# Operands split in place in a two-tile ring, and an earlier, closer-spaced preparation of the combined weights

## The chip, the cores and the metric

One NeuronCore of a Trainium2 chip runs the whole program in one launch. The metric is the device time of one execution in microseconds (us); several executions give a median. The engines are TensorE (PE, the matmuls; PEld is its weight load), VectorE (DVE), ScalarE (ACT), GpSimd (POOL) and SyncE (SP), whose queue issues nearly all DMAs.

## The reference

Three layers follow one another, all in float32: rotary attention (4 batches, 8 heads, 576 tokens, head size 64), then a layer with a maximum of three products, then one with SiLU.

```python
attn_out = _attn_ref(q, k, v)                                    # 4 x 8 x 576 x 64
x = attn_out.transpose(0, 2, 1, 3).reshape(2304, 512)
h = np.maximum(np.maximum(x @ w1, x @ w2), x @ w3)               # 512 -> 768
x = h @ w_out                                                    # 768 -> 512
h = x @ w_in                                                     # 512 -> 2048
out = (h * (1 / (1 + np.exp(-h)))) @ w_out2                      # 2048 -> 512
```

## The kernel before

A product of float32 operands is made of three float16 passes: each operand is scaled and split into a high and a low half, and the passes are high by high, high by low and low by high. ACT makes the high half, DVE the low half (`split`, L154 to L163).

**The stages.** Attention and the first layer (`moe1`) run interleaved until 610 us; then only the first layer's last batch is left, which is called the tail here: for its 576 tokens in two halves (256 and 320 columns) `up` makes 18 groups of matmuls each (3 matrices by 6 blocks of 128 hidden features), and `down` 4 groups of 18 passes each, over the 6 blocks. A group is one PSUM bank (`group`, L529). In the tail 7 banks are open to groups: 2 of `ps_m` and 5 of `ps_g`. ACT moves the first matrix's product out, DVE takes the maximum with the other two (L551, L553), ACT and DVE split the result (L559, L560), which `down` reads. `down` writes y to DRAM (`yscr`, L578).

**The second layer** (`moe2`, L827) takes tokens in 9 blocks of 256. Block 0 is computed plainly: `s1` (four units of 48 passes) makes h, `g_split` (L844) forms sums on POOL and splits, `s2` multiplies with the output weights. The other eight blocks go in four pairs J, each product of two by two sub-blocks being made from 7 products in place of 8 (`PRODUCTS`, L822). For this the operands need combined forms: sums and differences of sub-blocks. Of y they are made per J: `y7_load` (four DMAs), `y7_max` (largest magnitude, one DVE reduction), `y7_sums` (scales, and four differences on POOL, L937) and `y7_forms` (seven splits, L944, into the pool `y7_p`). `s1_pair` (8 of them, p = 0 to 7, per J) multiplies them with the combined input weights; between them stand units of `s2` (`second`).

**The combined weights** are prepared in the tail by `prep_steps` (L763), 16 items: 8 of the input weights ("wi", k = 0 to 7), 8 of the output weights ("wo", k = 8 to 15). An item loads two pieces from DRAM into a float32 tile of the ring `z7_p`, which has 3 tiles (L781); POOL makes four sums or differences in it (L785); ACT and DVE split it in two halves, forms 0 (or 1) to 3 and 4 to 7 (`high` L793, `low` L799). A "wi" item is written into a tile of the ring `w8o` (2 tiles of 8 forms) and by one DMA into DRAM (`w8scr`, L804); a "wo" item stays in SBUF as `w7`. Later `w8_load` (L1161) brings the "wi" forms back into one of four tiles, the first two of them early (L1180).

**The order.** `prep_steps` is a generator that is stepped once per group of the tail. Item k has its sums at step at0 + 3.4 k, its load 5 steps before, `high` and `low` of the first half 1 and 2 steps after, of the second 4 and 5 after; at0 is 6. Steps left at the tail's end are taken between the units of `s1` (`rest_step`). At the tail's first step block 0 of y is loaded into a tile of `z7_p` and split (L1175, L1176). A scheduler orders each engine's queue when the program is built, by this order as priority and by its own estimate of when each instruction can start; on the chip each queue runs in its order.

Of the kernel before, what the change touches and what calls it, by code (L numbers as in the profile page):

```python
# [17 lines left out]
P = 128  # L18
# [4 lines left out]
def fused_kernel(  # L23
# [502 lines left out]

    ps_g, wide_n = [], [0]

    def group(passes, n):  # L529

        wide_n[0] += 1
        ring, tag = (ps_g[0], "mg") if ps_g and wide_n[0] % 7 > 1 else (ps_m, "m")
        ps = ring.tile([P, 512], F32, tag=tag, name=tag)
        for i, (l, r) in enumerate(passes):
            nc.tensor.matmul(ps[:, 0:n], l, r, start=(i == 0), stop=(i == len(passes) - 1))  # L535
        return ps

    def moe1(b, pools):
# [33 lines left out]
        def down(half):  # L572
            o, n = PARTS[half][:2]

            def evac(m, ps):
                ysb = pools[2].tile([P, n], F32, tag="y", name="y")
                last["ma"] = nc.scalar.activation(out=ysb, in_=ps[:, 0:n], func=AF.Copy, scale=cy_t[b]).ins
                nc.sync.dma_start(out=yscr[:, m, b * S + o:b * S + o + n], in_=ysb)  # L578

            for m in range(KC):  # L580
                passes = []
                for f in range(NF1):
                    wh = WO1.h(f)[:, m * P:(m + 1) * P]
                    wl = WO1.l(f)[:, m * P:(m + 1) * P]
                    h = h1[half, f]
                    passes += [(wh, h[:, 0]), (wh, h[:, 1]), (wl, h[:, 0])]
                yield half, n * len(passes), True
                ps = group(passes, n)
                evac(m, ps)


        ahead = int(b > 0)
# [170 lines left out]
    def prep_steps(stage, out_p, w7_p, w7, at0, step):  # L763
# [7 lines left out]
        def item(k):  # L771
            nm, f = ("wi", k) if k < HB else ("wo", k - HB)
            z, w = {}, {}
            lo = 0 if nm == "wi" else 1

            def load():
                z[0] = stage.tile([P, 8, 256], F32, tag="z7", name="z7")
                for i in range(2):
                    o = (f + i * HB) * DM
                    x = zscr[nm][:, o:o + DM].rearrange("p (a n) -> p a n", a=2)  # L780
                    nc.sync.dma_start(out=z[0][:, i:i + 3:2] if nm == "wi" else z[0][:, 2 * i:2 * i + 2], in_=x)  # L781

            def sums():
                for o, x, y, op in SUMS if nm == "wi" else [d + (ALU.subtract,) for d in DIFFS]:
                    nc.gpsimd.tensor_tensor(out=z[0][:, o], in0=z[0][:, x], in1=z[0][:, y], op=op)  # L785
                if nm == "wi":
                    w[0] = out_p.tile([P, 2, 8, 256], F16, tag="w8o", name="w8o")
                else:
                    w[0] = w7[f] = w7_p.tile([P, 2, 7, 256], F16, name=f"w7{f}")

            def high(a, b):
                with tc.issue_after(last["ma"]):
                    nc.scalar.activation(  # L793
                        out=flat(w[0][:, 0, a - lo:b - lo]), in_=flat(z[0][:, a:b]), func=AF.Copy, scale=sc[nm]
                    )

            def low(a, b):
                with tc.issue_after(last["mv"]):
                    nc.vector.scalar_tensor_tensor(  # L799
                        out=flat(w[0][:, 1, a - lo:b - lo]), in0=flat(z[0][:, a:b]), scalar=sc[nm],  # L800
                        in1=flat(w[0][:, 0, a - lo:b - lo]), op0=ALU.mult, op1=ALU.subtract,
                    )
                if b == 8 and nm == "wi":
                    nc.sync.dma_start(out=w8scr[:, f], in_=w[0])  # L804
                    done8.append(f)

            t = at0 + k * step
            for d, fn in ((-5, load), (0, sums), (1, lambda: high(lo, 4)), (2, lambda: low(lo, 4)), (4, lambda: high(4, 8)), (5, lambda: low(4, 8))):
                steps.append((t + d, fn))
# [15 lines left out]
    )  # L825

    def moe2(st, pools, rings, ps_a, wo_rest, w7, w8_load):  # L827
        z_p, yr_p, y7_p, ga_p, sum_p, g7_p, tm_p, o_p = pools
        co_t, g7, acc, sc, gB, gA, ready = {0: st["y0"][3]}, {}, {}, {}, {}, {}, {}
        sg_t = {0: st["y0"][1]}  # L830
        nb = NT // 256
# [105 lines left out]
                nc.gpsimd.tensor_tensor(out=r[:, o], in0=r[:, x], in1=r[:, y], op=ALU.subtract)  # L937
            return s, ch

        def y7_forms(J, r, s, ch):  # L940
            forms = {}
            for _, _, _, b in PRODUCTS:
                t = forms[b] = y7_p.tile([P, 2, 2, 256], F16, tag=f"y7{b}", name=f"y7{b}")
                split(flat(t[:, 0]), flat(t[:, 1]), r[:, b + 1], s)  # L944
            sc[J] = forms, ch

        def s2(jb, u):
            if u == 0:
# [21 lines left out]
        def close(jb):  # L970
# [2 lines left out]
            co = small.tile([P, 1], F32, tag="co", name="co")  # L973
            nc.vector.tensor_scalar(out=co, in0=co_t[jb], scalar1=2.0 ** 25, scalar2=st["wo"].inv, op0=ALU.mult, op1=ALU.mult)
            ob = o_p.tile([P, 5, 256], F32, tag="ob", name="ob")
            tm = o_p.tile([P, 4, 256], F32, tag="tm", name="tm")
            add = lambda o, x, y: nc.vector.scalar_tensor_tensor(out=o, in0=x, scalar=co, in1=y, op0=ALU.mult, op1=ALU.add)
            nc.scalar.activation(out=tm[:, 0], in_=b[:, 0], func=AF.Copy, scale=co)
            add(ob[:, 0:3:2], a, tm[:, 0:1].to_broadcast([P, 2, 256]))
# [58 lines left out]
        for J in range(nb // 2):  # L1038
            A, B = 1 + 2 * J, 2 + 2 * J
            more = J + 1 < nb // 2  # L1040
            for p in range(HB):
                s1_pair(J, p)
                splits()
                if p == 1 and more:
                    raw = y7_load(J + 1)
                if p == 4 and more:
                    m = y7_max(raw)
                if p == 5:
                    todo.append((A, 0))
                    if more:  # L1050
                        sums = y7_sums(J + 1, raw, m)
                if p == HB - 1:
                    if more:
                        y7_forms(J + 1, raw, *sums)
# [137 lines left out]
    moe2(st, pools2, ((ps_m, "m"), (ps_b, "mb")), ps_a, chain, w7, lambda k: early.get(k) or w8_load(k))  # L1192

# [42 lines left out]
```

## Time and profile before

| | us |
|---|---|
| median of 3 runs | 1049.69 |
| lowest, highest | 1047.83, 1053.84 |
| the profiled execution, its own time | 1046.5 |
| its span in the trace | 1044.8 |
| PE busy (modelled), share of the span | 963.2, 92% |
| DVE busy | 691.1, 66% |
| ACT busy | 614.4, 59% |
| POOL busy | 496.3, 48% |

Busy time of PE is modelled from the issue of matmuls that overlap in its pipeline, so its idle time is the part that tells something; its granted clock has two levels here, 1.00 (2.4 GHz) and 0.50 (1.2 GHz), and a mean between them is a stretch with both. In all rows times are from the span's start.

### The profile page before, as it was taken

The page shows a single profiled execution, that of the slowest core. Times are in us where ns is not written, and L with a number is a line of the kernel's source. Part 1 is how long each engine was busy: PE and PEld are TensorE (multiplying, and loading weights), DVE is VectorE, ACT ScalarE, POOL GpSimd, SP SyncE. Part 2 cuts the span into 40 slices and gives each one's busy share as a digit, 9 for nine tenths or more (in the row PEclk, how much of TensorE's full clock was granted, in tenths as well). Part 3 has the DMA queues.
Part 4 walks back from the last instruction along what each step waited for, and adds up shares of the span by engine and source line. Part 5 has one row for each costly group of instructions (what it writes and reads, how often), then busy time and mean ns, then how long its engine had stood idle before and what let it go on. Part 6 is the DMA issues. An engine that isn't in the chain of part 4 may idle for free.

```text
span 1044.8 us, 19296 instructions
## 1 busy us (share of the span) xinstructions
PE 963.2 (92%) x7234; PEld 719.5 (69%) x7234; DVE 691.1 (66%) x1279; ACT 614.4 (59%) x1361; POOL 496.3 (48%) x516
## 2 busy tenths in 40 slices
PE   4677989999989999999999999897998999999997
PEld 2343665666665766667766577686787887888886
DVE  6769878344578566486556656877668678577554
ACT  3778677556766666667666844474454544555442
POOL 6735592920136541051111126989357438347254
PEclk9688999999999999999999999999899999999999
DMA  6943131300334522233233229884244344332201
GB/s 151 278 114 100 33 95 37 105 2 13 102 94 128 143 83 73 73 94 91 67 92 104 89 72 327 268 317 146 94 139 132 123 144 128 113 127 92 85 9 41
DMA packets 103277, 117.98 MB, mean 113 GB/s; under 512 B 46096, under 2 KB 75536, under 8 KB 102160
## 3 DMA queue, kind: packets, MB, share of 16 engines
q1 hardware_dynamic: 101680, 116.03, 36.3%
q8 instruction: 57, 0.93, 0.4%
q10 hardware_dynamic: 1504, 0.72, 0.3%
q14 instruction: 36, 0.29, 0.1%
HBM read 90.51 MB, written 26.21 MB: 112 GB/s over the span
## 4 chain that ended last, share of the span: by engine, by line
PE 63%; DVE 10%; POOL 6%; DMA 5%; ACT 4%; issue 3%; SPq 1%; DVEq 0%; POOLq 0%; ACTq 0%
PE m L535 19%; PE m L902 7%; PE xp L466 6%; PE s L389 5%; PE mb L902 5%; PE tr L447 5%; POOL z L785 3%; PE b L966 3%; PE a L966 3%; PE c L966 3%; POOL gsum L849 2%; PE d L966 1%; PE xp L462 1%; DMA z<-zwi 1%; PE s L386 1%
## 5 line engine op out<-in xcount | busy, mean ns | idle before, releaser
L535 PEld LDWEIGHTS <-w 128*128 128x128 f16 x1632 | 158.2, 98 | 64.3 <-issue 23.5
L535 PE MATMUL m<-x,w 128*128 128x256 f16 (+1 forms) x1336 | 189.9, 287 | 11.5 <-DVE t L553 5.0
L211 POOL TENSOR_SCALAR z<-z 128x256 uint16<-128x256 uint16 x64 | 54.4, 850 | 244.6 <-DVE z L210 236.4
L966 PEld LDWEIGHTS <-g 128*128 128x128 f16 x1485 | 145.1, 98 | 19.7 <-ACT g L853 1.7
L902 PEld LDWEIGHTS <-w8s 128*128 128x128 f16 x1344 | 132.7, 99 | 32.4 <-issue 14.6
L399 DVE TENSOR_REDUCE nb<-s 128x2 f32<-128x1152 f32 (+1 forms) x80 | 98.7, 1234 | 63.0 <-PE s L389 44.2
L406 ACT ACTIVATE e<-s,nb 128x576 f32<-128x576 f32 x144 | 105.3, 737 | 36.6 <-DVE nb L399 27.7
L418 ACT ACTIVATE e<-e,rec 128x576 f32<-128x576 f32 x144 | 104.2, 768 | 17.3 <-DVE rec L416 17.1
L447 PE MATMUL tr<-ident,e 128*128 128x128 f32 x576 | 96.2, 288 | 13.3 <-ACT T L349 6.1
L902 PE MATMUL m<-y,w8s 128*128 128x256 f16 x768 | 93.6, 278 | 13.0 <-DVE t L908 8.1
L447 PEld LDWEIGHTS tr<-ident,e 128*128 128x128 f32 x576 | 70.0, 147 | 45.2 <-issue 12.3
L785 POOL TENSOR_TENSOR z<-z 128x256 f32<-128x256 f32 x64 | 68.6, 1096 | 38.2 <-DMA z<-zwi 37.0
L466 PE MATMUL xp<-pt,vd 128*64 128x256 f32 (+1 forms) x512 | 82.6, 418 | 0.0
L389 PE MATMUL s<-T 64*128 64x512 f32 x256 | 82.3, 687 | 0.0
L451 ACT ACTIVATE pt<-tr 128x384 f32<-128x384 f32 x119 | 56.3, 486 | 39.1 <-PE tr L447 38.5
L916 POOL TENSOR_TENSOR z<-t 128x256 f32<-128x256 f32 x32 | 28.0, 876 | 88.2 <-DVE t L908 52.6
L902 PE MATMUL mb<-y,w8s 128*128 128x256 f16 x576 | 69.2, 274 | 0.7 <-DVE ga L908 0.7
L535 PE MATMUL m<-h,wo 128*128 128x256 f16 (+1 forms) x448 | 66.8, 291 | 0.1
L535 PEld LDWEIGHTS <-wo 128*128 128x128 f16 x512 | 49.7, 99 | 24.3 <-issue 10.7
L854 DVE SCALAR_TENSOR_TENSOR g<-gsum,sg,g 128x1024 f16<-128x1024 f32 x36 | 50.6, 1411 | 18.0 <-ACT g L853 17.5
L329 POOL TENSOR_TENSOR w<-qk,sin_sb 128x384 f32<-128x384 f32 (+1 forms) x44 | 45.1, 1045 | 36.4 <-DMA qk<-in_q_dram 21.2
L853 ACT ACTIVATE g<-gsum,sg 128x1024 f16<-128x1024 f32 x36 | 40.7, 1140 | 33.6 <-POOL gsum L849 33.6
(229 smaller groups left out, 1902.1 us busy)
## 6 DMA issues: line engine op xcount, KB each, us to landing
w8s<-w8scr SPq DMA_DIRECT2D x32, 896.0 KB, 4.7
z<-in_moe_w_in_dram SPq DMA_DIRECT2D x32, 256.0 KB, 3.2
z<-in_moe_w_out_dram SPq DMA_DIRECT2D x32, 256.0 KB, 3.2
w8scr<-w8o SPq DMA_DIRECT2D x8, 1024.0 KB, 5.3
w<-in_moe_w_dram SPq DMA_DIRECT2D x6, 768.0 KB, 5.4
wo<-in_moe_w_dram SPq DMA_DIRECT2D x6, 768.0 KB, 4.6
qk<-in_q_dram SPq DMA_DIRECT2D x32, 128.0 KB, 3.2
vd<-in_v_dram SPq DMA_DIRECT2D x16, 256.0 KB, 3.1
```

Of the source, the lines that this page charges most:

```text
L211: nc.gpsimd.tensor_scalar(out=q[:, :, 2], in0=q[:, :, 1], scalar1=step, scalar2=off, op0=ALU.mult, op1=ALU.add)
L389: last["s"] = nc.tensor.matmul(s[:, o:o + 512], qs[r], kt[r], start=True, stop=True).ins
L399: x = nc.vector.tensor_reduce(out=nb[:, 0:m], in_=both(s, 0, 960, 576) if m > 1 else s[:, 0:576], op=ALU.max, axis=AX.X, negate=True)
L406: x = nc.scalar.activation(out=e[:, HK[g]], in_=s[:, SK[g]], func=AF.Exp, bias=nb[:, g:g + 1], accum_out=sm[:, g:g + 1])
L418: nc.scalar.activation(out=e[:, HK[g]], in_=e[:, HK[g]], func=AF.Copy, scale=r[:, g:g + 1])
L447: nc.tensor.transpose(tr[:, i * n:(i + 1) * n], e[0:n, c * P:(c + 1) * P], ident[0:n, 0:n])
L451: nc.scalar.activation(out=to, in_=of, func=AF.Copy)
L466: nc.tensor.matmul(xp[r, 0:n], v4[:, g, c, :], pt[:, c + 5 * g, :], start=False, stop=(c == 3))
L535: nc.tensor.matmul(ps[:, 0:n], l, r, start=(i == 0), stop=(i == len(passes) - 1))
L785: nc.gpsimd.tensor_tensor(out=z[0][:, o], in0=z[0][:, x], in1=z[0][:, y], op=op)
L902: nc.tensor.matmul(o, l, r, start=(i == 0), stop=(i == len(passes) - 1))
L966: x = nc.tensor.matmul(ps, l, r, start=first, stop=last_, skip_group_check=True)
```

## The change

Five things are changed.

1. In the tail's second half, `down` opens its four groups with the passes of hidden blocks 0 to 4 and adds block 5's three passes to each afterwards; all four results are moved out after that.
2. `prep_steps` starts with at0 = 1 and has a step of 3.0. "wi" items use `w8o` tiles of half the size (4 forms), of which there are still 2, and each half is written to DRAM by its own DMA.
3. Block 0 of y is loaded at the tail's step 12 and split at step 16, in place of step 0.
4. Three tiles of `w8s` are loaded early, in place of two; the fourth comes from the space that the tail leaves.
5. `y7_p` is gone. A form's two float16 halves are written into the float32 tile `yr` itself: form b's into slot b, from slot b + 1. There are two `yr` tiles. Load, maximum and sums of J + 1 stand at p = 0, 1 and 2 (before: 1, 4 and 5), and the forms at p = 3 to 7 (1, 1, 2, 2 and 1 of them; before all 7 at p = 7). The temporary of `close` comes from the ring of `s1_pair`'s (2 tiles) in place of its own.

```diff
-    def group(passes, n):
+    def group(passes, n, ps=None, more=False):
...
         for i, (l, r) in enumerate(passes):
-            nc.tensor.matmul(ps[:, 0:n], l, r, start=(i == 0), stop=(i == len(passes) - 1))
+            nc.tensor.matmul(ps[:, 0:n], l, r, start=(first and i == 0), stop=(not more and i == len(passes) - 1))
...
+            open_ = []
             for m in range(KC):
...
-                ps = group(passes, n)
-                evac(m, ps)
+                if ps_g and half:
+                    k = len(passes) - 3
+                    open_.append((m, passes[k:], group(passes[:k], n, more=True)))
+                else:
+                    evac(m, group(passes, n))
+            for m, passes, ps in open_:
+                evac(m, group(passes, n, ps))
...
             def high(a, b):
+                if nm == "wi":
+                    w[a] = out_p.tile([P, 2, 4, 256], F16, tag="w8o", name="w8o")
...
-                if b == 8 and nm == "wi":
-                    nc.sync.dma_start(out=w8scr[:, f], in_=w[0])
-                    done8.append(f)
+                if nm == "wi":
+                    nc.sync.dma_start(out=w8scr[:, f, :, a:b], in_=w[a])
+                    if b == 8:
+                        done8.append(f)
...
-        def y7_forms(J, r, s, ch):
-            forms = {}
-            for _, _, _, b in PRODUCTS:
-                t = forms[b] = y7_p.tile([P, 2, 2, 256], F16, tag=f"y7{b}", name=f"y7{b}")
-                split(flat(t[:, 0]), flat(t[:, 1]), r[:, b + 1], s)
-            sc[J] = forms, ch
+        def y7_forms(J, r, s, ch, lo_hi=range(7)):
+            for b in lo_hi:
+                t = r[:, b].bitcast(F16)
+                split(t[:, 0:512], t[:, 512:1024], r[:, b + 1], s)
+            if lo_hi[-1] == 6:
+                sc[J] = [r[:, b].bitcast(F16).rearrange("p (x c n) -> p x c n", x=2, c=2) for b in range(7)], ch
...
-            tm = o_p.tile([P, 4, 256], F32, tag="tm", name="tm")
+            tm = tm_p.tile([P, 4, 256], F32, tag="t1", name="t1")
...
+                if p == 0 and more:
+                    raw = y7_load(J + 1)
                 if p == 1 and more:
-                    raw = y7_load(J + 1)
-                if p == 4 and more:
                     m = y7_max(raw)
+                if p == 2 and more:
+                    sums = y7_sums(J + 1, raw, m)
+                if p > 2 and more:
+                    y7_forms(J + 1, raw, *sums, lo_hi=((0,), (1,), (2, 3), (4, 5), (6,))[p - 3])
...
-    chain = prep_steps(z7_p, w8o_p, w7_p, w7, 6, 3.4)
+    chain = prep_steps(z7_p, w8o_p, w7_p, w7, 1, 3.0)
...
-        if n == 0:
+        if n == 12:
             y0 = y_load(0, z7_p.tile([P, 8, 256], F32, tag="z7", name="z7")[:, 0:4].rearrange("p a n -> p (a n)").rearrange("p (a n) -> p a n", n=512), 256)
+        if n == 16:
             st["y0"] = y_split(y0, yt_p, st)
...
-            for k in range(2):
+            for k in range(3):
                 early[k] = w8_load(k)
...
-    w8b = Ring(ctx, "w8b", 2)
-    w8r += [w8b, w8b]
+    w8r.append(Ring(ctx, "w8b", 1))
...
-        for nm, bufs in (("yr_p", 1), ("y7_p", 1), ("ga_p", 3), ("sum_p", 2), ("g7_p", 3), ("tm_p", 2), ("o_p", 1))
+        for nm, bufs in (("yr_p", 2), ("ga_p", 3), ("sum_p", 2), ("g7_p", 3), ("tm_p", 2), ("o_p", 1))
```

## Rows read from the trace of the kernel before

**Rows 1.** Windows: from-to, length, busy us (instructions) per engine, clock, DMA share, GB/s.

```profile
610.40:666.40 56.00, 56.00 (x459) 44.85 (x460) 41.11 (x59) 28.73 (x44) 35.85 (x36) 1.00 0.76 257
666.40:681.20 14.80, 11.80 (x75) 7.74 (x73) 10.25 (x12) 6.97 (x10) 14.34 (x15) 0.88 0.67 225
681.20:709.60 28.40, 26.94 (x245) 23.56 (x243) 23.35 (x28) 20.48 (x27) 23.87 (x22) 1.00 0.79 281
709.60:733.40 23.80, 15.05 (x122) 12.20 (x121) 17.94 (x16) 9.18 (x11) 21.45 (x17) 0.91 0.45 160
733.40:738.70 5.30, 5.28 (x25) 3.77 (x26) 0.87 (x3) 1.72 (x3) 2.00 (x2) 0.50 0.00 0
738.70:782.40 43.70, 43.70 (x397) 38.88 (x396) 29.33 (x60) 22.34 (x36) 19.33 (x23) 0.99 0.41 139
782.40:804.00 21.60, 18.22 (x160) 15.01 (x158) 17.84 (x28) 10.40 (x19) 16.98 (x17) 1.00 0.40 135
862.00:892.00 30.00, 27.59 (x253) 24.28 (x251) 23.42 (x30) 15.35 (x23) 26.13 (x27) 1.00 0.40 117
```

**Rows 2.** Timeline of PE at the tail's end: start, us, instruction, [idle before, releaser].

```profile
669.06 0.43 PE L535 MATMUL mg<-h,wo 128*128 128x320 f16 x2 [0.72 <-DVE h L560]
...
673.54 0.70 PE L535 MATMUL mg<-h,wo 128*128 128x320 f16 x4 [2.28 <-ACT h L559]
...
674.35 3.73 PE L535 MATMUL m<-h,wo 128*128 128x320 f16 x14
```

**Rows 3.** Timeline of PE, ACT, DVE, 709 to 739 us; PE's wait on `w8s`.

```profile
715.79 1.01 PE L902 MATMUL m<-y,w8s 128*128 128x256 f16 x4 [4.68 <-ACT ga L871]
...
733.42 5.28 PE L902 MATMUL m<-y,w8s 128*128 128x256 f16 x24 [4.06 <-DVE t L908]
...
714.01 1.15 ACT L793 ACTIVATE w<-z,wohalf 128x1024 f16<-128x1024 f32 x1 [5.98 <-POOL z L785]
...
730.67 2.27 DVE L149 TENSOR_REDUCE ym<-yr 128x1 f32<-128x2048 f32 x1
...
PE m L870 <- DMA w8s<-w8scr: 1.5, 1, 1.5
```

**Rows 4.** Windows on POOL, 681.2 to 726.6 us: L785 (sums), L849 (gsum), L937 (yr).

```profile
681.20:726.60 45.40, 18.40 (x15) 0.96 0.68 242
...
681.20:726.60 45.40, 17.16 (x16) 0.96 0.68 242
...
681.20:726.60 45.40, 5.82 (x5) 0.96 0.68 242
```

**Rows 5.** Timeline of POOL in the tail: the sums, with the idle time before.

```profile
615.67 6.82 POOL L785 TENSOR_TENSOR z<-z 128x256 f32<-128x256 f32 x8 [22.78 <-DMA z<-zwi]
631.59 10.90 POOL L785 TENSOR_TENSOR z<-z 128x256 f32<-128x256 f32 x12 [9.10 <-DMA z<-zwi]
```

**Rows 6.** Groups in the tail; DMA issues (KB, us to landing); last, the `w8s` loads' landing.

```profile
L799 DVE SCALAR_TENSOR_TENSOR w8o<-z,wihalf,w8o 128x1024 f16<-128x1024 f32 x16 | 22.6, 1430 | 9.0 <-ACT w8o L793 9.0
L793 ACT ACTIVATE w8o<-z,wihalf 128x1024 f16<-128x1024 f32 x16 | 18.1, 1143 | 15.7 <-DMA w8scr<-w8o 7.3 <-POOL z L785 5.6 <-DMA z<-zwi 2.0
...
w8scr<-w8o SPq DMA_DIRECT2D x8, 1024.0 KB, 5.3
...
w8s<-w8scr SPq DMA_DIRECT2D x8, 512.0 KB, 5.7
...
DMA to landing us min/median/max: 3.8/5.7/7.9
```

**Rows 7.** The y forms' groups, 681 to 740 us; DVE's wait on `yr`; ACT's on POOL.

```profile
L162 DVE SCALAR_TENSOR_TENSOR y<-yr,sh,y 128x512 f16<-128x512 f32 x7 | 7.7, 1166 | 0.0
...
L157 ACT ACTIVATE y<-yr,sh 128x512 f16<-128x512 f32 x7 | 4.4, 708 | 1.8 <-DVE sh L743 1.8
...
796.44 2.29 DVE L149 TENSOR_REDUCE ym<-yr 128x1 f32<-128x2048 f32 x1 [1.38 <-DMA yr<-yscr]
...
ACT z L920 <- POOL z L916: 7.0, 4, 4.4
```

More of the change, by code (lines that the diff above doesn't have):

```diff
@@ L527, in fused_kernel @@
     ps_g, wide_n = [], [0]
-    def group(passes, n):
-        wide_n[0] += 1
-        ring, tag = (ps_g[0], "mg") if ps_g and wide_n[0] % 7 > 1 else (ps_m, "m")
-        ps = ring.tile([P, 512], F32, tag=tag, name=tag)
+    def group(passes, n, ps=None, more=False):
+        first = ps is None
+        if first:
+            wide_n[0] += 1
+            ring, tag = (ps_g[0], "mg") if ps_g and wide_n[0] % 7 > 1 else (ps_m, "m")
+            ps = ring.tile([P, 512], F32, tag=tag, name=tag)
         for i, (l, r) in enumerate(passes):
-            nc.tensor.matmul(ps[:, 0:n], l, r, start=(i == 0), stop=(i == len(passes) - 1))
+            nc.tensor.matmul(ps[:, 0:n], l, r, start=(first and i == 0), stop=(not more and i == len(passes) - 1))
         return ps
@@ L785, in sums, with high @@
                     nc.gpsimd.tensor_tensor(out=z[0][:, o], in0=z[0][:, x], in1=z[0][:, y], op=op)
+                if nm == "wo":
+                    w7[f] = w7_p.tile([P, 2, 7, 256], F16, name=f"w7{f}")
+                    w[0], w[4] = w7[f][:, :, 0:3], w7[f][:, :, 3:7]
+            def high(a, b):
                 if nm == "wi":
[L787 to L791, printed above, removed]
+                    w[a] = out_p.tile([P, 2, 4, 256], F16, tag="w8o", name="w8o")
                 with tc.issue_after(last["ma"]):
                     nc.scalar.activation(
-                        out=flat(w[0][:, 0, a - lo:b - lo]), in_=flat(z[0][:, a:b]), func=AF.Copy, scale=sc[nm]
+                        out=flat(w[a // 4 * 4][:, 0]), in_=flat(z[0][:, a:b]), func=AF.Copy, scale=sc[nm]
                     )
             def low(a, b):
+                h, l = (flat(w[a // 4 * 4][:, i]) for i in range(2))
                 with tc.issue_after(last["mv"]):
                     nc.vector.scalar_tensor_tensor(
-                        out=flat(w[0][:, 1, a - lo:b - lo]), in0=flat(z[0][:, a:b]), scalar=sc[nm],
-                        in1=flat(w[0][:, 0, a - lo:b - lo]), op0=ALU.mult, op1=ALU.subtract,
-                    )
-                if b == 8 and nm == "wi":
-                    nc.sync.dma_start(out=w8scr[:, f], in_=w[0])
-                    done8.append(f)
+                        out=l, in0=flat(z[0][:, a:b]), scalar=sc[nm], in1=h, op0=ALU.mult, op1=ALU.subtract
+                    )
+                if nm == "wi":
+                    nc.sync.dma_start(out=w8scr[:, f, :, a:b], in_=w[a])
+                    if b == 8:
+                        done8.append(f)
             t = at0 + k * step
@@ L827, in moe2 @@
     def moe2(st, pools, rings, ps_a, wo_rest, w7, w8_load):
-        z_p, yr_p, y7_p, ga_p, sum_p, g7_p, tm_p, o_p = pools
+        z_p, yr_p, ga_p, sum_p, g7_p, tm_p, o_p = pools
         co_t, g7, acc, sc, gB, gA, ready = {0: st["y0"][3]}, {}, {}, {}, {}, {}, {}
@@ L1043, in moe2 @@
                 splits()
+                if p == 0 and more:
+                    raw = y7_load(J + 1)
                 if p == 1 and more:
-                    raw = y7_load(J + 1)
-                if p == 4 and more:
                     m = y7_max(raw)
+                if p == 2 and more:
+                    sums = y7_sums(J + 1, raw, m)
+                if p > 2 and more:
+                    y7_forms(J + 1, raw, *sums, lo_hi=((0,), (1,), (2, 3), (4, 5), (6,))[p - 3])
                 if p == 5:
                     todo.append((A, 0))
-                    if more:
-                        sums = y7_sums(J + 1, raw, m)
                 if p == HB - 1:
-                    if more:
-                        y7_forms(J + 1, raw, *sums)
                     todo += [(A, u) for u in range(1, UNITS)] + [(B, u) for u in range(UNITS)]
@@ L1156, in fused_kernel @@
     right_p = lambda nm, bufs: Ring(ctx, nm, bufs, side="right")
-    z7_p, w7_p, yt_p, w8a = right_p("z7_p", 3), right_p("w7_p", 1), right_p("yt_p", 1), right_p("w8a", 2)
+    z7_p, w7_p, yt_p, w8a = right_p("z7_p", 3), right_p("w7_p", 1), right_p("yt_p", 1), right_p("w8a", 3)
     w8o_p = Ring(left, "w8o", 2)
-    w7, w8r = {}, [w8a, w8a]
+    w7, w8r = {}, [w8a] * 3
     def w8_load(k):
```

## The prediction

> **What bounds the kernel now.** I read the windows first, because 92% of PE busy is a mean over stages. In the tail up to 666.4 us, and again from 738.7 to 782.4 us, PE has no idle time at the full clock [rows 1]: there the matmuls are the bound, and the change takes none away. What can be won is PE's lost time. It stands in four places [rows 1]: 666.4 to 681.2 us, 14.80 less 11.80 = 3.0 us idle, and a mean clock of 0.88, so 24% of 14.8 us at the half clock, where half is lost: 1.8 us; 681.2 to 709.6 us, 1.5 us idle; 709.6 to 738.7 us, 8.75 us idle, about 2.1 us by the clock of 0.91 and 2.5 us in a stretch wholly at 0.50 (25 matmuls in 5.28 us, against 0.11 us each before and after); 782.4 to 804 and 862 to 892 us, 3.4 and 2.4 us idle. Together 25.5 us, which is all that this change could bring.
>
> The timeline says why. At the tail's end PE has opened two `down` groups and then waits 0.72 and 2.28 us for the last two hidden blocks, and runs on at half clock (14 matmuls in 3.73 us) [rows 2]. At 711 us PE waits 4.68 us for SiLU, since ACT stood 5.98 us before a `high` whose sums POOL had not made; at 729 us it waits 4.06 us for DVE, which was behind the splits of `gsum` and a 2.27 us maximum [rows 3]. Both lead back to POOL: from 681.2 to 726.6 us it is busy 18.4 + 17.2 + 5.8 = 41.4 of 45.4 us, with 15 left-over weight sums, the sums of block 0 and the first differences of y [rows 4]. So POOL sets the end of this stage.
>
> **The change part by part.**
>
> *Groups of `down` held open.* No instruction is added. Four groups of 15 passes stand before block 5 is needed, two more than the scheduler opened by itself. A pass costs 11.80 us over 75, about 0.14 us at the full clock [rows 1], so 30 more passes give 4.2 us of cover for a wait of 2.28 us. The 0.72 us stay, since block 4 is among the first 15. The half-clock stretch followed the idle time and goes with it: 4.1 us in all. The four evictions now come together and share two y tiles; the third waits for a DMA, and behind it only the second layer's first bank. I cost that at 0: the other bank is ready. If not, it costs one landing, some 5 us. PE then reaches the second layer at 677 us.
>
> *Preparation of the weights.* It adds 8 DMA issues on SP, where nothing waits long. Two things pull. For it: POOL stood idle 9.10 us before item 2, whose tile held y [rows 5]; with y later, items 0 to 2 follow without a gap. At the 0.85 us of the first sums (6.82 us for 8 [rows 5]) 64 sums are 55 us, and at the 1.23 us of the later ones (18.4 over 15 [rows 4]) 79 us; from 615 us on, fed without a gap, they would end between 670 and 694 us, and the two POOL waits of rows 3 would vanish. Against it: `w8o` has half its space. Now a tile's cycle is two `high` (1.14 us each), two `low` (1.43) and 5.3 us to landing, 10.4 us [rows 6], and with two tiles an item passes every 5.2 us. ACT already waited 7.3 us for this DMA [rows 6]. Afterwards each half has one tile: 1.14 + 1.43 + the landing of 512 KB. No row has such a write; the nearest are reads of that size, 3.8 us at least and 5.7 in the median [rows 6], and below nothing cannot come. The cycle is thus 6.4 to 8.3 us for an item; I take 7.3, midway, since the median stems from a stretch with the DMA engines at 0.76 to 0.79 [rows 1] and fewer bytes per us will then be moving.
>
> The row first: 512 KB landed no faster than 1 MB (5.7 against 5.3 us [rows 6]). The Trainium skill (DMA: Bandwidth & Descriptors, Bandwidth) asks for batches of 1 MiB or more and so speaks against halving this write. Its fit (Anatomy of one DMA; a fixed 2.0 us plus bytes at 436 GB/s, measured there on GpSimd's path) gives an estimate of 3.2 us, a cycle of 5.8 us and an end of the "wi" items some 10 us sooner than my value does; no run here shows it, and I go by the rows.
>
> With 7.3 us: first load landed at 615, four sums 3.4 us, one `high` and one `low`, 621 us for item 0, and 7 x 7.3 more: 672 us for item 7, where it needed about 666 (8 items of 5.2 us, and the 9.10 us gap). Meanwhile POOL is not lost: the tile that y leaves early carries items 8, 11 and 14 ahead, while 9 and 10 wait for the tiles of items 6 and 7. By 677 us I count 12 items (0 to 9, 11, 14) summed, 16 sums left. Then POOL's end is 677 + 16 x 1.23 + 17.2 + 5.8 us, and idle time between none and the 4.0 us of now: 719.7 to 723.7, say 721.7 where it was 726.6. That is 5 us sooner, and it already holds the 4.1 us of the tail, which alone would only make PE wait longer. I add 1.7 us, since the 4.68 us wait before a late sum shrinks and with it part of the half-clock stretch. With a cycle of 6.4 us the items end 6 us sooner and six fewer sums are left: 7 us more gain. With 8.3 us and an ACT or DVE queue in the way by 1 us each time, 24 sums are left at 677 us and POOL ends at 677 + 29.5 + 23 + 4 = 733.5 us, 7 us later than now.
>
> *Third early `w8s`.* Its gain is at most the 1.5 us that PE waited for these loads [rows 3]; I take 1.5, because fewer loads crowd into the same stretch.
>
> *Forms in place.* The work is the same: 7 `high` of 0.63 and 7 `low` of 1.10 us, 4.4 and 7.7 us [rows 7]. But form b's `high` now waits for the `low` of form b - 1, which reads its slot: 7 x 1.73 = 12.1 us plus hand-overs, not 8 to 9. For the pairs J = 1 to 3 that lies over five pairs of p and costs nothing as long as DVE is not full there. What it removes is the block of 7.7 us on DVE at p = 7, and with two tiles the load of `yr` no longer waits for the last form: DVE stood 1.38 us before a 2.29 us maximum for it [rows 7]. Of the 5.8 us idle at the two boundaries I take 4.3 off (bounds 0 and 5.8); the rest is POOL's sums. For J = 0 the seven stand together, and the second product needs form 5, which was made second and now comes sixth: 4 x 1.73, 7 us later, before which PE has the units of `s2` of block 0. I charge 1.5 us (bounds 0 and 7).
>
> *`close` in the ring of `s1_pair`* makes a pair's first eviction wait for POOL's add two tiles back. ACT's waits on that add are 7.0 us in 4 cases [rows 7], off PE's path; I charge 0, at most 2 us.
>
> Sum: -5 - 1.7 - 1.5 - 4.3 + 1.5 = -11 us against the profiled execution's 1046.5, so 1035.5. The median is 3.2 us above that execution; against it the forecast is 1038.7 us.
>
> **The rivals.** *Full feed:* the write lands at 3.8 us or less, POOL is done by 700 us, both waits of rows 3 go. Gain 4.1 + 1.5 + 13.4 less some 2, and 4.3 at the boundaries: 21 us, 1028.7. For it speaks POOL's idle time in the tail; against it ACT's waits on the larger `w8o`. *Swallowed:* the cycle is near 7.9 us, POOL ends at 726 as now, the tail's gain turns into a wait at 711 us, the third early load brings nothing, and only the boundaries, less the chain of forms, remain: -4.3 + 1.5, 1046.9. *Slower, by the half tiles:* from a cycle of about 8.3 us and a blocked queue on, POOL ends 7 us later, PE waits that long and 2.5 us more at half clock: 9.5 - 4.3 = +5.2, 1055. What speaks for it is that the larger tiles already held ACT up for 7.3 us [rows 6]; against it, that POOL has two tiles to run ahead in. The Trainium skill's rule on batches (above) points the same way. That the change does not do what it says I see only for the groups: the scheduler opened two by itself.
>
> **How the numbers follow.** Forecast 0.48 (itself 1033 to 1043), full feed 0.20, swallowed 0.18, slower 0.14. A measurement of this kernel can tell about 0.5%, 5.2 us. Faster 0.68, same 0.18, slower 0.14. The range from 1027 to 1051 leaves out the slow case and the best end of full feed.
>
> **What would show it.** Right: no idle time above 1 us on PE before `down`'s last passes; `w8scr` writes of one half 7 us apart; POOL's last weight sum before 715 us; no `ym` wait on `yr`, and under 2 us idle at the boundaries. Wrong: writes of one half 8.3 us or more apart and PE idle beyond 730 us; or PE waiting 3 us and more for forms before the first pair.

## The result and the profile after

| | before | after |
|---|---|---|
| median of 14 runs each, us | 1049.3 | 1058.12 |
| lowest, highest | 1047.31, 1054.15 | 1054.01, 1062.23 |
| span of the profiled execution | 1044.8 | 1057.6 |
| start of the last eviction of attention (`t0`) | 610.5 | 613.5 |
| span less `t0`, called **rest** below | 434.3 | 444.1 |

The ratio is 1.0076, 95% interval 1.0058 to 1.0094: slower, where faster was forecast, and above the range. Up to the end of attention both programs issue the same instructions in the same order, and still `t0` lies between 609.4 and 617.8 us over the 17 profiles of this study. It is no part of the change, so everything below counts from `t0`. Each rest is that of one profiled execution; two kernels that were profiled twice gave rests 0.7 and 0.1 us apart, and the first of them PE busy times 1.7 us apart (405.12 and 406.85, the same matmuls at another clock), so differences of rests below some 2 us are not told apart here.

The windows of after, with the columns of [rows 1], in the same stages:

```profile
613.50:669.50 56.00, 46.57 (x372) 37.17 (x371) 29.41 (x49) 22.95 (x36) 22.64 (x28) 0.91 0.67 217
669.50:693.80 24.30, 22.32 (x161) 15.59 (x160) 17.77 (x21) 12.67 (x18) 18.92 (x18) 1.00 0.71 236
693.80:712.70 18.90, 11.84 (x91) 9.74 (x90) 11.61 (x9) 12.44 (x17) 18.74 (x18) 0.82 0.75 245
712.70:740.00 27.30, 22.90 (x189) 18.66 (x188) 22.54 (x25) 13.81 (x18) 27.30 (x23) 0.94 0.65 223
785.00:810.00 25.00, 25.00 (x231) 22.40 (x229) 19.87 (x28) 15.37 (x26) 18.64 (x19) 1.00 0.49 157
860.00:900.00 40.00, 39.07 (x359) 34.82 (x357) 27.07 (x40) 17.04 (x26) 28.32 (x32) 1.00 0.47 149
```

The first 56 us of the tail, without idle time and at the full clock before [rows 1], now have 9.43 us idle and a mean clock of 0.91; the tail ends 80.3 us after `t0`, where it took 70.9. The first 19 us behind it have 7.06 us idle at 0.82. Added up, the idle times in PE's timeline are 25.6 us up to 165 us after `t0` (before 13.2) and 3.6 us at the two boundaries behind (before 6.1): 9.9 us more, for a rest 9.8 us longer. PE's modelled busy time behind `t0` is 409.4 us in both, so the loss is idle time. PE's waits from the tail on, and the largest in its timeline:

```profile
PE m L116 <- DVE ym L149: 12.3, 2, 9.4
PE mb L880 <- ACT y L579: 7.1, 1, 7.1
PE m L912 <- DVE t L918: 2.9, 3, 1.4
PE m L912 <- ACT yr L157: 2.8, 1, 2.8
```

```profile
659.24 0.37 PE L116 MATMUL m<-ident,ym 128*1 128x128 f32 x1 [9.43 <-DVE ym L149]
...
685.16 0.43 PE L537 MATMUL mg<-h,wo 128*128 128x320 f16 x2 [1.59 <-DVE h L562]
...
700.87 6.11 PE L880 MATMUL mb<-yt,w8s 128*128 128x256 f16 x36 [7.06 <-ACT y L579]
...
743.95 0.28 PE L912 MATMUL m<-yr,w8s 128*128 128x256 f16 x1 [2.84 <-ACT yr L157]
```

Of these four only the second was there before, as the wait of 0.72 us [rows 2]. The 4.68 us wait for SiLU and the 2.28 us wait at the tail's end [rows 2, 3] are gone; in their place PE's queue stands behind a transpose of the maximum of y, and at the second layer's start behind the eviction of y. That eviction stands on ACT behind three `high` of the weights, which wait for POOL:

```profile
697.20 2.80 ACT L802 ACTIVATE w<-z,wohalf 128x1024 f16<-128x1024 f32 x3 [2.50 <-POOL z L793]
699.90 0.92 ACT L579 ACTIVATE y<-mg,cy 128x320 f32<-128x320 f32 x2
```

What is late on ACT and POOL: the writes of the combined input weights as SP issues them, their issue group, ACT's waits in the tail, and POOL's sums.

```profile
619.98 0.36 SPq L813 DMA_DIRECT2D w8scr<-w8o  x1
...
625.50 1.11 SPq L813 DMA_DIRECT2D w8scr<-w8o  x2
...
678.90 2.59 SPq L813 DMA_DIRECT2D w8scr<-w8o  x2
688.97 0.43 SPq L813 DMA_DIRECT2D w8scr<-w8o  x1
```

```profile
w8scr<-w8o SPq DMA_DIRECT2D x16, 512.0 KB, 5.6
```

```profile
ACT w8o L802 <- DMA w8scr<-w8o: 22.1, 8, 4.3
ACT w L802 <- POOL z L793: 6.5, 3, 3.7
```

```profile
639.39 2.90 POOL L793 TENSOR_TENSOR z<-z 128x256 f32<-128x256 f32 x4 [6.34 <-DMA z<-zwi]
648.78 2.89 POOL L793 TENSOR_TENSOR z<-z 128x256 f32<-128x256 f32 x4 [6.49 <-DMA z<-zwi]
664.84 2.91 POOL L793 TENSOR_TENSOR z<-z 128x256 f32<-128x256 f32 x4 [13.17 <-DMA z<-zwi]
...
722.16 0.73 POOL L793 TENSOR_TENSOR z<-z 128x256 f32<-128x256 f32 x1
```

The second halves' writes run from 625.50 to 688.97 us: seven cycles of 9.1 us. A write of half the size lands no sooner here (5.6 us, for 1 MB 5.3 [rows 6]). ACT waits 22.1 us for free `w8o` tiles (before 7.3 [rows 6]), and the last write is issued 75.5 us after `t0`, before 55.3 (665.76 us). POOL is not fed without a gap: while the tiles wait for ACT, the next loads come late, and it stands 6 to 13 us before single items. Its last weight sum ends 109.4 us after `t0`, before 109.9: POOL's end did not move; what stands in the queues ahead of it did.

### The profile page after: what moved, and what is told of

Read it like the earlier page. It is cut to its first block, busy times and chain, and to the rows that moved or that the text cites. A ratio compares the mean times of both kernels' runs of the same rounds, so it can differ in the third digit from the quotient of the medians.

```text
span 1057.6 us, 19321 instructions
## 1 busy us (share of the span) xinstructions
PE 966.2 (91%) x7234; PEld 720.4 (68%) x7234; DVE 688.0 (65%) x1279; ACT 617.8 (58%) x1361; POOL 491.9 (47%) x516
## 4 chain that ended last, share of the span: by engine, by line
PE 61%; DVE 9%; DMA 7%; POOL 7%; ACT 5%; issue 3%; SPq 2%; DVEq 0%; ACTq 0%; POOLq 0%
PE m L537 18%; PE xp L466 6%; PE m L912 5%; PE s L389 5%; PE tr L447 5%; PE mb L912 4%; POOL gsum L859 3%; DMA w8scr<-w8o 3%; PE c L976 3%; PE b L976 3%; PE a L976 2%; POOL z L793 2%; PE xp L462 1%; DVE g L864 1%; PE d L976 1%
## 5 line engine op out<-in xcount | busy, mean ns | idle before, releaser
L537 PE MATMUL m<-x,w 128*128 128x256 f16 (+1 forms) x1336 | 192.2, 290 | 12.7 <-DVE t L555 6.3
L406 ACT ACTIVATE e<-s,nb 128x576 f32<-128x576 f32 x144 | 105.4, 738 | 36.7 <-DVE nb L399 28.0
L447 PE MATMUL tr<-ident,e 128*128 128x128 f32 x576 | 96.5, 288 | 13.6 <-ACT T L349 6.2
L912 PE MATMUL m<-yr,w8s 128*128 128x256 f16 x768 | 90.8, 273 | 5.8 <-DVE t L918 2.9
L793 POOL TENSOR_TENSOR z<-z 128x256 f32<-128x256 f32 x64 | 62.0, 993 | 58.1 <-DMA z<-zwi 55.1
L912 PE MATMUL mb<-yr,w8s 128*128 128x256 f16 x576 | 69.1, 273 | 0.0
L466 PEld LDWEIGHTS xp<-pt,vd 128*64 128x64 f32 x512 | 36.5, 138 | 33.0 <-issue 14.5
```

The costliest lines, as they stand in the source:

```text
L406: x = nc.scalar.activation(out=e[:, HK[g]], in_=s[:, SK[g]], func=AF.Exp, bias=nb[:, g:g + 1], accum_out=sm[:, g:g + 1])
L447: nc.tensor.transpose(tr[:, i * n:(i + 1) * n], e[0:n, c * P:(c + 1) * P], ident[0:n, 0:n])
L466: nc.tensor.matmul(xp[r, 0:n], v4[:, g, c, :], pt[:, c + 5 * g, :], start=False, stop=(c == 3))
L537: nc.tensor.matmul(ps[:, 0:n], l, r, start=(first and i == 0), stop=(not more and i == len(passes) - 1))
L912: nc.tensor.matmul(o, l, r, start=(i == 0), stop=(i == len(passes) - 1))
```

## The experiments

All the runs (rest, the tail's end and the first pair's start, all in us from `t0`; medians in us; the ratio is that of the record, against before's runs beside each kernel, whose medians lie between 1049.2 and 1050.7, and so not the quotient of two medians of this table; "halves 2" is after's ring of two half tiles, "halves 4" the same space as before's):

| kernel | parts | rest | tail's end | first pair | median | ratio [95%] |
|---|---|---|---|---|---|---|
| before | none | 434.3 | 70.9 | 99.2 | 1049.3 | 1 |
| after | all | 444.1 | 80.3 | 117.8 | 1058.12 | 1.0076 [1.0058, 1.0094] |
| e1_y0_first | all, y at step 0 | 443.2 | 79.5 | 115.1 | 1057.77 | 1.0066 [1.0041, 1.0092] |
| e2_four_halves | all, halves 4 | 432.2 | 78.4 | 115.3 | 1046.2 | 0.9967 [0.9951, 0.9984] |
| e3_forms_alone | 5 | 430.1 | 70.9 | 99.0 | 1044.47 | 0.9963 [0.9939, 0.9987] |
| e4_open_alone | 1 | 428.5 | 66.8 | 96.5 | 1041.11 | 0.9909 [0.9883, 0.9934] |
| e5_open_and_forms | 1, 5 | 431.4 | 66.8 | 106.3 | 1047.36 | 0.9985 [0.9966, 1.0004] |
| e6_halves_only | 1, 5, halves 2, three early loads | 435.8 | 73.6 | 107.4 | 1050.54 | 1.0013 [0.9992, 1.0033] |
| e7_halves_with_space | 1, 5, halves 4 | 428.7 | 67.1 | 103.1 | 1045.1 | 0.9956 [0.9935, 0.9976] |
| e8_y0_first_four_halves | 1, 5, halves 4, start and step | 433.7 | 80.3 | 116.8 | 1048.73 | 1.0002 [0.9985, 1.0019] |
| e9_two_early | all, two early loads | 443.2 | 77.6 | 122.0 | 1058.79 | 1.0081 [1.0051, 1.0111] |
| e10_open_and_rate | 1, start and step | 435.8 | 80.8 | 108.9 | 1051.09 | 1.001 [0.9987, 1.0033] |
| e11_open_again | 1 | 427.8 | 66.8 | 96.8 | 1041.35 | 0.9922 [0.9892, 0.9952] |
| e12_open_and_forms_again | 1, 5 | 431.5 | 67.5 | 106.4 | 1045.53 | 0.9951 [0.9931, 0.9971] |
| e13_open_start | 1, start | 436.5 | 75.3 | 105.9 | 1051.78 | 1.0023 [1.0003, 1.0043] |
| e14_open_step | 1, step | 432.2 | 74.0 | 100.8 | 1048.72 | 0.9994 [0.9972, 1.0016] |
| e15_open_four_halves | 1, halves 4 | 426.6 | 66.7 | 94.2 | 1039.89 | 0.9908 [0.9879, 0.9938] |

**Is it where y is split?** The largest wait, 9.43 us, stands before the transpose of y's maximum, so the first suspicion fell on the move of y to steps 12 and 16.

```diff
-        if n == 12:
+        if n == 0:
             y0 = y_load(0, ...)
-        if n == 16:
             st["y0"] = y_split(y0, yt_p, st)
```

> The changed kernel with block 0 of y loaded and split at the tail's step 0 again; all else as changed. Theory A (the wait of 9.43 us on PE for block 0's maximum is what the change costs): that wait and the half clock behind it go, about 11 us less than the changed kernel, ratio to before near 0.998. Theory B (the two half-size w8o tiles set the pace of the preparation, and whatever is late shows up later on POOL and ACT): the wait goes, but the items still close some 9 us apart, POOL's last weight sum is no earlier, and PE waits instead at the tail's end and before the first pair; at most 4 us less, ratio near 1.004.

The wait is gone, and the rest is 0.9 us shorter, no more. PE's timeline and ACT's wait in this kernel:

```profile
680.22 0.43 PE L537 MATMUL mg<-h,wo 128*128 128x320 f16 x1 [5.66 <-ACT h L561]
...
698.89 6.35 PE L880 MATMUL mb<-yt,w8s 128*128 128x256 f16 x34 [6.35 <-ACT y L579]
```

```profile
ACT w8o L802 <- DMA w8scr<-w8o: 20.8, 6, 5.8
```

ACT still stands 20.8 us before free tiles, and PE now waits for what is queued on ACT behind that: the splits of h. The wait that the profile names first was a symptom.

**The space of `w8o`.** Four half tiles, the space of before, with the third early tile given back; and, so that this second edit can be told from the first, after with two early loads alone.

```diff
-    ... w8a = ..., right_p("w8a", 3)
-    w8o_p = Ring(left, "w8o", 2)
+    ... w8a = ..., right_p("w8a", 2)
+    w8o_p = Ring(left, "w8o", 4)
...
-            for k in range(3):
+            for k in range(2):
...
```

(e9: without the two lines of `w8o`; in both the ring of the later `w8s` tiles gets the tile back)

> The changed kernel with four half-size w8o tiles (the space that before had), and for it two early w8s tiles instead of three; block 0 of y stays at steps 12 and 16. Theory B: the items close about 5 us apart as before, POOL is fed, the wait for block 0's maximum shrinks to under 3 us since its load's place on SP comes sooner, and the time falls by 10 us or more from the changed kernel, ratio to before 0.998 or less. Theory A: the wait on PE for block 0's maximum stays at 7 us or more, and the time falls by at most 4 us, ratio near 1.004.

> The changed kernel with two early w8s tiles in place of three (two later ones), the two half-size w8o tiles kept. SP stands 15.3 us before the three early loads in the changed kernel, since each waits for the write it reads, and item loads stand behind them. If that is what stretches the items to some 9 us: writes 7 us apart or less, 5 us or more gained, ratio near 1.002. Theory B (the half tile's own cycle of split, write and landing, 9 us): writes still 8 to 9 us apart and the ratio stays at 1.005 to 1.008.

e9 is like after, so the third early load is worth nothing here. Nor do SP's waits before the three early loads, 15.3 us, stretch the items by way of the third: in e9 8.5 us of them are left, and its writes of second halves are 8.7 us apart (the two other loads were not moved). e2 and e9 differ in nothing but the ring: 432.2 against 443.2, **11.0 us for half the space**. e2's ACT waits and its POOL timeline:

```profile
ACT w L802 <- POOL z L793: 13.1, 6, 3.0
...
ACT w8o L802 <- DMA w8scr<-w8o: 2.5, 1, 2.5
```

```profile
660.34 36.69 POOL L793 TENSOR_TENSOR z<-z 128x256 f32<-128x256 f32 x32 [1.47 <-DVE co L984]
```

The wait for the maximum of y is 1.45 us here. With space ACT waits 2.5 us for the writes, and POOL makes its last 32 weight sums in one stretch: done at 697.0 us, 84 us after `t0` instead of 109. This is what the forecast hoped for. Still the tail ends at 78.4, not at 66.8 as in e4: something else holds it.

The same question at the old start and step, with and without the space:

```diff
-    chain = prep_steps(z7_p, w8o_p, w7_p, w7, 1, 3.0)
+    chain = prep_steps(z7_p, w8o_p, w7_p, w7, 6, 3.4)
```

(with y at step 0; e7 has e2's edit besides)

> The changed kernel with the preparation's order as before (first sums at step 6, 3.4 groups for an item, block 0 of y at step 0), but with the two half-size w8o tiles and three early w8s tiles; against open_and_forms only these two differ. Theory B (half the space sets the pace): the items close about 9 us apart all the same and the time stays near the changed kernel's, ratio 1.004 or more. Theory C (the early start and closer spacing put ACT and SP in a bad order, and the half tiles are harmless with the order of before): ratio near that of open_and_forms, under 0.993.

> The same with four half-size tiles and two early w8s tiles: the halved DMAs with the space of before. Theory B: as open_and_forms within 0.3%. If a write of half the size costs by itself (16 issues in place of 8): 3 us or more above it.

e6's wait, and e7's:

```profile
ACT w8o L802 <- DMA w8scr<-w8o: 7.6, 7, 2.1
```

```profile
ACT w8o L802 <- DMA w8scr<-w8o: 0.4, 1, 0.4
```

Here half the space costs 435.8 - 428.7 = 7.1 us, 6.5 of them in the tail (e6 has the third early load besides, worth nothing in e9). But neither theory's case came in e6: the ratio is between theirs, and the items close 6.8 us apart, not 9. Its writes, issued 1.7 us or more after one another, also land sooner than after's, most of which go out in pairs 0.6 to 2.2 us apart:

```profile
w8scr<-w8o SPq DMA_DIRECT2D x16, 512.0 KB, 3.1
```

So the 9.1 us of after come from half the space together with the early start and the closer spacing (e1, 8.7 us; e2, with the space, 6.0), not from half the space alone. Sixteen writes of 512 KB at full space cost nothing: e7 is 2.7 us shorter than e5, which has eight of 1 MB. That is no gain either: it lies in PE's busy time (405.6 against 408.5 us), and e12, the same program as e5, has nearly e7's median (1045.53 and 1045.1).

**Start and step.** Parts 1 and "at0 = 1, step 3.0" with the full tiles, then each of the two by itself; and e2 with y at step 0, which beside e7 has the start and the step alone.

```diff
-    chain = prep_steps(z7_p, w8o_p, w7_p, w7, 6, 3.4)
+    chain = prep_steps(z7_p, w8o_p, w7_p, w7, 1, 3.0)
```

(e13: 1, 3.4; e14: 6, 3.0; e8: e7 with 1, 3.0)

> The kernel before with part 1 and the preparation's early start and closer spacing, full-size w8o tiles, two early w8s tiles, block 0 of y at step 0. Against open_alone it shows start and spacing by themselves. If an earlier end of POOL's sums is worth its cost to the tail: ratio below that of open_alone (0.991) by 0.002 or more. If the splits, now in front of the tail's evictions on ACT and DVE, lengthen the tail by as much as POOL's earlier end gives back: 0.991 to 0.997.

> Part 1 and the early start alone (first sums at step 1, 3.4 groups for an item, full-size w8o tiles). Start and spacing together made the stage behind attention 7 us longer than part 1 alone (435.8 against 428.5 us) and the tail 14 us (80.8 against 66.8). If the early start does it, since splits of the first items then stand before the first evictions: the tail stays at 75 us or more, ratio near 1.000. If the spacing does it: the tail is within 3 us of 66.8, ratio 0.990 to 0.994.

> Part 1 and the closer spacing alone (first sums at step 6, 3.0 groups for an item). The other side of the same question: tail 75 us or more and ratio near 1.000 if the spacing does it, tail within 3 us of 66.8 and ratio 0.990 to 0.994 if it is the start.

> Early start and spacing of 3.0 kept, four half-size tiles, two early w8s tiles, block 0 of y at step 0. Against four_halves (0.9967, y late) it shows what y's place costs when the items are not throttled: nothing if ratio 0.995 to 0.998; 3 us or more if 0.993 or less. Against halves_with_space it shows what start and spacing are worth: POOL ends sooner, so 2 to 6 us less, if POOL is the bound before the first pair; the same or more if the evictions behind the weights' splits on ACT take it back.

Against e4 the rest grows by 7.3 us for both, 8.0 for the start and 3.7 for the step; against e7, by 5.0 for both. They do not add up, but each costs by itself (e10 came out slower than both of its cases, and e14's tail 1 us short of the 75 us that it named), and where: the tail's end goes from 66.8 to 80.8, 75.3 and 74.0, in e8 from 67.1 to 80.3. e10's wait on ACT (in e4 this line is 5.3 us in 2) and its PE; then, of e13 and of e14, PE's wait for an h and ACT before that h:

```profile
ACT w8o L801 <- POOL z L793: 13.6, 5, 3.3
```

```profile
660.08 9.30 PE L537 MATMUL mg<-x,w 128*128 128x320 f16 x48 [4.72 <-ACT y L579]
...
683.74 0.69 PE L537 MATMUL mg<-h,wo 128*128 128x320 f16 x2 [2.62 <-DVE h L562]
```

```profile
677.60 0.43 PE L537 MATMUL mg<-h,wo 128*128 128x320 f16 x1 [2.82 <-ACT h L561]
...
673.97 1.97 ACT L801 ACTIVATE w<-z,wohalf 128x1024 f16<-128x1024 f32 x2 [2.62 <-POOL z L793]
677.07 0.47 ACT L561 ACTIVATE h<-t 128x320 f16<-128x320 f32 x1 [1.13 <-DVE t L555]
```

```profile
677.26 2.83 PE L537 MATMUL mg<-h,wo 128*128 128x320 f16 x10 [3.64 <-ACT h L561]
...
674.88 1.97 ACT L801 ACTIVATE w<-z,wohalf 128x1024 f16<-128x1024 f32 x2 [1.75 <-POOL z L793]
676.76 0.45 ACT L561 ACTIVATE h<-t 128x320 f16<-128x320 f32 x1
```

The steps put `high` and `low` into ACT's and DVE's queues at the group where the sums are taken to be ready. Nearer together they are not: ACT stands before a `high`, and the evictions and splits of the tail, which PE needs, are behind it. In all, ACT's waits for POOL's sums in the 80 us from `t0` are 10.6 us in e4, 17.0 in e10, 15.6 in e13 and 12.0 in e14. What it gains lies behind the tail: from the tail's end to 130 us after `t0` the idle times of PE add up to 7.2 us in e8, to 13.3 in e7. But in the tail they are 10.4 us against 1.0. y at step 0 or later makes 1.5 us (e8 against e2), the other way round than in after, and e8's ratio is outside both cases named for it: no clear effect.

**Part 1 by itself**, twice. Its edit is the change's diff from `group` to the last `evac`.

> The kernel before with part 1 alone: the last hidden block's passes of the four down groups held back. The prediction: the wait of 2.28 us and the half clock go (4.1 us), but POOL's end pins the stage, so the gain turns into a longer wait near 711 us: ratio 0.998 to 1.000. If the tail's end is on the path by itself: 0.996. If the four evictions together delay the second layer's first bank by a DMA landing: 1.001 or more.

> The same kernel as open_alone, beside the next on one chip: 0.991 if that result holds, 0.995 if it was one of the chip's better stretches.

The windows of e4, with the columns of [rows 1], and PE's largest waits in them; then the second of these waits in e11, the same program:

```profile
614.40:674.40 60.00, 59.26 (x482) 47.07 (x482) 45.14 (x65) 31.37 (x48) 40.18 (x40) 1.00 0.79 264
674.40:714.40 40.00, 31.38 (x265) 25.47 (x263) 31.21 (x34) 26.86 (x36) 35.68 (x33) 1.00 0.84 286
714.40:744.40 30.00, 28.25 (x258) 25.17 (x258) 26.45 (x30) 13.62 (x19) 27.37 (x24) 1.00 0.35 114
```

```profile
673.05 0.43 PE L537 MATMUL mg<-h,wo 128*128 128x320 f16 x2 [0.74 <-DVE h L562]
684.24 2.78 PE L878 MATMUL mb<-yt,w8s 128*128 128x256 f16 x24 [3.01 <-ACT y L579]
```

```profile
679.20 4.25 PE L878 MATMUL mb<-yt,w8s 128*128 128x256 f16 x24 [3.01 <-ACT y L579]
```

The tail ends 4.1 us sooner, to the tenth what was forecast: the 0.7 us wait stays, the 2.28 us wait and the half clock behind it [rows 2] go. Behind it the eviction, of which the forecast had said that it would cost nothing, holds PE for 3.01 us. Still the gain is not swallowed: the rest is 5.8 and 6.5 us shorter, the ratios are 0.9909 and 0.9922, below all three of the cases expected. The waits of 4.68 and 4.06 us [rows 3] are gone, the largest left is 3.01; idle time up to 130 us after `t0` is 11.1 us in e4 and 9.2 in e11 (before 13.2). Over the whole rest PE is idle 1.4 and 3.9 us less; the other part of the gain is PE's busy time, 405.1 and 406.9 us in place of 409.4, since less of it is at the half clock. POOL, too, is done sooner. In its timeline 8 weight sums are left behind the long block of them that ends 78 us after `t0`, in e4 and in e11; before, 12 were left behind the block that ended at 74 us, and the last ends 105.7 and 107.6 us after `t0`, not 109.9. That fits the shorter waits; that it causes them was not tried by itself.

**Part 5 by itself, and behind part 1**, the second twice. Its edit is the change's diff from `y7_forms` to `close` and the last hunk.

> The kernel before with part 5 alone: forms in place, two yr tiles, load, maximum, sums and forms spread over p = 0 to 7, close's temporary in the pairs' ring. The prediction had 4.3 us less at the pairs' boundaries and 1.5 us more before the first pair: ratio 0.997. If the serial chain of the seven first forms or the shared temporary costs what the boundaries bring: 1.000. If POOL's sums, not the forms, make the idle time at the boundaries: 3 us or more stay idle there, and the ratio is 1.000 to 1.002.

> The kernel before with parts 1 and 5, and none of the weights' preparation changed. If the two gains add (0.9909 and 0.9963 each alone): 0.987. If they share one slack, POOL's end before the first pair: 0.991.

> The same kernel as open_and_forms: 0.998 if the gains of the groups and of the forms really do not add; 0.990 or less if the difference was between chips.

Alone it shortens the rest by 4.2 us, close to what was expected; behind part 1 it lengthens it by 2.9 and 3.7 us (e5 to e4, e12 to e11), which none of the cases expected of e5 and e12 had. PE in e3; then the forms on ACT, first in e4 (seven in one block) and then in e5 (the first and the last):

```profile
721.79 0.37 PE L902 MATMUL mb<-yr,w8s 128*128 128x256 f16 x1 [5.62 <-ACT yr L157]
```

```profile
707.33 4.40 ACT L157 ACTIVATE y<-yr,sh 128x512 f16<-128x512 f32 x7 [0.17 <-DVE sh L751]
```

```profile
712.68 0.72 ACT L157 ACTIVATE yr<-yr,sh 128x512 f16<-128x512 f32 x1 [2.02 <-DVE sh L751]
...
721.05 0.72 ACT L157 ACTIVATE yr<-yr,sh 128x512 f16<-128x512 f32 x1 [1.38 <-DVE yr L162]
...
735.63 0.72 ACT L157 ACTIVATE yr<-yr,sh 128x512 f16<-128x512 f32 x1 [1.14 <-DVE yr L162]
```

In place the seven forms of J = 0 go to and fro between ACT and DVE, with other work of both queues between: 23.7 us from first to last on ACT, in place of 4.4. In e3 PE waits 5.62 us for one, 105.4 us after `t0`; but before's 4.68 us wait [rows 3] stood at this very place (105.3 us), and it and the 4.06 us wait behind it go. e3's idle time up to 130 us is thus no shorter than before's (13.7 against 13.2 us); it gains 2.1 us at the later boundaries and 3.1 us in PE's busy time (406.3 in place of 409.4), at less half clock. e4 had removed the two waits already, so that behind it the chain's cost stands alone: the first pair begins at 106.3, not at 96.5. At the later boundaries PE's idle time falls from 6.7 us (e4) to 3.5 (e5). How much of the cost is the chain itself, and how much the load and the maximum of J = 1, which now stand ahead of these forms, was not tried.

**Part 1 with half tiles at full space**, to see whether anything of part 2 pays.

```diff
-    w8o_p = Ring(left, "w8o", 2)
+    w8o_p = Ring(left, "w8o", 4)
```

(on e4, with the change's `sums`, `high` and `low`)

> Part 1 with the preparation's order of before, and four half-size w8o tiles written by sixteen DMAs. With the forms in place the same step took the stage behind attention from 431.4 to 428.7 us. If that gain is the writes' own: 426 us and a ratio of 0.988 or less, the fastest kernel here. If it only made good what the forms cost: as part 1 alone, 0.991.

It is 1.9 us shorter than e4 in the rest and 1.2 than e11, and has e4's ratio, 0.9908: the best two kernels, not to be told apart by their times, and both faster than before and after.

The path from before to after, in us of the rest, where steps below some 2 us, and the step of e7, are not clear of the noise: part 1 -5.8, part 5 +2.9 (e5), half tiles at full space -2.7 (e7), half the space with the third early tile +7.1 (e6), start and step +7.4 (e1), y's place +0.9: together +9.8, as measured.

## Why the prediction was wrong

**What bounds the kernel** was read rightly as to the stages: all that moved lies in the stretches of [rows 1] that it named, or in the tail before them. Wrong was that the tail up to 666.4 us could not get worse: it had no idle time, and so was given no term. The tail lost 9.4 us (70.9 to 80.3), though part 1 took 4.1 off its end.

**Groups held open**: 4.1 us forecast, 4.1 us at the tail's end and about 6 in the rest measured. That this gain alone would only make PE wait longer, for POOL, was wrong (e4, e11): it took POOL's end as fixed, and with part 1 alone POOL ended 2.3 to 4.2 us sooner. The path of the "swallowed" rival falls with it.

**Preparation of the weights** is the step that failed: the -5 - 1.7 us of the sum (4.1 of the 5 are the tail's), which priced the halved space and the early, closer-spaced items by POOL's end alone. *The cycle*: 7.3 us taken, bounds 6.4 to 8.3, 9.1 measured. The half tiles by themselves keep the forecast: in e6, in before's order, the items close 6.8 us apart, and the last write is issued 62.6 us after `t0`, where the forecast's 672 us are 61.6. With the early start and the closer spacing it is 8.7 us and 74.8 (e1), 9.1 and 75.5 (after). So the cycle was worked out for an order that the change did not keep; what in the new order stretches it, the writes' landing in pairs or the queues of ACT, DVE and SP, stays open. *Where the cost lands*: POOL's end was to come 5 us sooner. It did not move (109.4 against 109.9 us), and the price was paid by what stands behind a waiting `high` in ACT's queue, and behind the transposes of y in PE's. *Start and step* were counted only as a gain: e10, e13 and e14 show a loss of 3.7 to 8.0 us with the full tiles, e8 one of 5.0. In place of the gain of 2.6 us that this leaves for the preparation, the runs show a cost of 7.1 to 11.0 us by the space (e6 against e7, e9 against e2) and of 3.7 to 8.0 us by start and step.

On the size of a write: 512 KB took 5.6 us to landing in after and 3.1 in e6, 1 MB 5.3 [rows 6]. The Trainium skill (DMA: Bandwidth & Descriptors, Bandwidth) asks for batches of 1 MiB or more; for the single write the trace agrees, since half the bytes took more than half the time in both. For the kernel no price of it shows where there is space (e5 to e7, e4 to e15). The fit of the Trainium skill (DMA: Bandwidth & Descriptors, Anatomy of one DMA) gave an estimate of 3.2 us; it is stated for GpSimd's path, but e6's 3.1 us, on SP's, agree with it, and after's 5.6 us do not.

**Third early load**: 1.5 us forecast, none measured (e9).

**Forms in place**: -4.3 + 1.5 = -2.8 us forecast, -4.2 measured alone (e3), but +2.9 and +3.7 behind part 1 (e5, e12). The boundaries gave 2.5 us in after (6.1 to 3.6 us idle) and 3.2 from e4 to e5, below the 4.3. DVE's wait for the load of `yr` did not go entirely:

```profile
881.38 2.29 DVE L149 TENSOR_REDUCE ym<-yr 128x1 f32<-128x2048 f32 x1 [0.80 <-DMA yr<-yscr]
```

It was 1.38 us [rows 7]. The chain of J = 0, for which 1.5 us was taken of bounds 0 to 7, costs nearer to the upper end once part 1 has taken away the wait that hid it: 2.9 us net plus the 3.2 of the boundaries, about 6, of which 2.9 are idle time and the others PE at the half clock (405.1 to 408.5 us busy). That all of it is the chain's was not tried.

**The rivals**: "slower, by the half tiles" (1055) had the sign, the half tiles and nearly the size. Its path was only in part right: not POOL ending 7 us later (that came in e6 and e1, 118.7 and 117.1 us after `t0`, with half the space and y at step 0), but ACT, DVE and PE standing in the tail itself. "Swallowed" had POOL's end right, and that the third early load brings nothing; its time, 1046.9, was 11 us too low. Of the signs of being wrong the first came: writes 9.1 us apart and PE idle beyond 730 us. The second did not quite: the wait of 2.84 us for a form is inside the first pair. Of the signs of being right none came.

## What to carry to other kernels

An instruction that is moved earlier in an in-order queue is free only if its inputs are there: where an engine feeds the critical path and prepares something else besides, look at what stands behind each preparing step, and not only at when the last of them ends. Halving a buffer's size with the count kept halves the run-ahead, which costs more than smaller transfers; halving the size and doubling the count cost nothing here. A cycle that is worked out from the rows of one order holds for that order: the same half tiles took 6.8 us an item in the old one and 9.1 in the new. When a change has five parts, measure the simplest by itself: part 1 alone is worth 0.8 to 0.9%, and the others took more than that away.

## What the hardware showed that was not expected

The same 512 KB write to DRAM, from the same ring, took 3.1 us to landing in the median in e6 and 5.6 in after, with the DMA engines at 0.75 (e6) and at 0.67 and 0.71 (after) in these stretches; 1 MB took 5.3, at 0.76. The load on the engines does not tell the two apart. The spacing might: in after's five closest pairs (0.6 to 1.2 us apart) each write took 4.1 to 7.0 us, and its first write, alone, 3.08. That was not tried by itself.

The clock behind one and the same wait is not always the same. In e4 and e11, one program, PE waits 3.01 us before 24 matmuls at the second layer's start; they take 2.78 us in one profile and 4.25 in the other (the lines stand under part 1), and e11's clock over those 10 us is 0.83, e4's 1.00. The rest of e11 is nevertheless the shorter by 0.7 us: its idle time up to 130 us after `t0` is 1.9 us less (9.2 against 11.1), perhaps since PE, slower, finds more of the next operands ready. So half clock that is read off a profile, as the forecast did for three stretches, is not all time to be won.
